# Block one's local attention takes q and k from the tiles that the pooled branch has already loaded

## The chip, the cores and the metric

The kernel runs on one core of a Trainium2 chip. The metric is the device time of one execution in microseconds (us), taken as the median of several runs; lower is better.

## The reference

The input is q, k and v of shape (4, 8, 576, 64): batch, heads, tokens, head size. Two attentions are added, and the sum goes through two feed-forward layers.

```
q_d, k_d, v_d = mean of q, k, v over groups of 4 tokens          # 144 pooled tokens
out_up    = repeat(softmax(q_d k_d^T / 8) v_d, 4 times)          # pooled branch
mask      = |i - j| < 4
out_local = softmax(where(mask, q k^T / 8, -1e9)) v              # local branch, a band of 7
x = (out_up + out_local) as (2304 tokens, 512)
h = x @ w_in1 (512 x 2048);  x = relu(h)^2 @ w_out1              # first layer
h = x @ w_in2;               out = (h * cos(h)) @ w_out2         # second layer
```

The two weight pairs come as 64-bit floats.

## The kernel before

Tokens are worked on in five blocks per layer; block one of the first layer has 512 tokens. For the first layer a slot is one of the 16 chunks of 128 hidden columns for one block: `stage_a` multiplies x by the chunk (L568), the activation follows, and `stage_b1` multiplies back into four accumulators (L620). Each operand is kept as a high part and a rest (`xh` and `xl`, `w1hi` and `loa`/`lob`, `gh` and `gl`), so a product is three matmuls.

**Attention.** Heads go in four pairs: heads 2p and 2p+1 lie on partitions 0-63 and 64-127. The pooled branch of a batch (`pool`) loads eight pieces of q and k (one per pair and tensor, 128 x 576) and four of v, and VectorE sums groups of four tokens (L260, L265, L267). `down` then makes pooled scores (L303), the exponentials on ScalarE (L277), transposes (L324, copies L331) and the product with v (L336, copies L345). The local branch goes by windows of 64 queries with up to 70 keys; block one has windows 0 to 7. `window` loads its own q and k (`qkw`, L367) and v (`vw`, L372). In `qkw` the two heads' queries stand side by side padded with zeros, so that one 128x128 weight tile gives the scores of both heads in one matmul per pair (L383), four per window, behind one matmul that writes the mask (L379). Then come the row maximum (L273), exponentials (L277), the scaling on GpSimd (L393), transposes (L403, copy L406), the product with v (L420), the sum with the pooled branch (L436), and its split in `xh` (L448) and `xl` (L449).

**Weights.** `conv1(f)` turns chunk f of the 64-bit weights into two 32-bit parts: the load `raw` (L461, two buffers), one pass on ScalarE (L475), four on VectorE (L477, L478, L482, L485), one on ScalarE that writes `w1hi` (L489), two on GpSimd (L496) and two stores (L521).

**Order.** Before the first slot all tasks of block one run in turn until they end (`early[0]` is true): `pool(0)`, its four `down`, windows 0 to 7, and the conversion of chunks 0 to 2; the warm-up matmuls (L697) stand between the turns. In that stretch the weight tiles `hi3` to `hi15` are still empty, and the buffers named in `SPREAD` use them: `need` takes an own buffer where there is one, or else one of the 13 empty tiles. A scheduler then sets the order on each engine, and each engine works its list strictly from front to back. SP issues all loads; all DMAs share the same 16 DMA engines.

Of the kernel before, what the change touches and what calls it, by code (L numbers as in the profile page):

```python
# [8 lines left out]
F32 = mybir.dt.float32  # L9
# [9 lines left out]
P = 128  # L19
B, H, S, D = 4, 8, 576, 64  # L20
# [3 lines left out]
HPAIR = H // 2  # L24
WQ = 64
WK = WQ + 2 * HALO
# [13 lines left out]
W0 = [sum(WINS1[:j]) for j in range(NB + 1)]  # L40
# [13 lines left out]
TOP_MIN = 2.0 ** -15  # L54
TOP_MAX = (2.0 - 2.0 ** -3 - 2.0 ** -23) * 2.0 ** 16
LO_RING = (("loa", AHEAD), ("lob", AHEAD + LAG))
SPREAD = ("pl", "qkw", "vw", "dpr", "dpt")
RANK = {"down": 0, "window": 1, "pool": 2, "conv1": 3, "conv2": 3}


# [8 lines left out]
def kernel(  # L69
# [43 lines left out]

    caps = {
        "a": 3, "h": 1, "acc": 4, "qkw": 3, "vw": 3, "pr": 3, "pt": 2, "xt": 1, "qp": 1, "xd": 2, "vp": 1, "av": 3, "pl": 2, "raw": 2,
        "dpr": 2, "dpt": 1,
    }
    used = dict.fromkeys(caps, 0)
    now = [-1]
# [3 lines left out]

    def need(name, n=1):
        while early[0] and name in SPREAD:
            if name != "pl" and used[name] < caps[name]:
                used[name] += 1
                held.setdefault(name, []).append(None)
                return
            if spare:  # L130
                held.setdefault(name, []).append(spare.pop(0))
                return
            yield
        while used[name] + n > caps[name]:
            yield
        used[name] += n

    def done(name, n=1):
        f = taken[name].pop(0) if early[0] and name in SPREAD else None
        if f is None:  # L140
            used[name] -= n
        else:
            spare.append(f)
# [4 lines left out]
    def task_tile(name, rows, cols):  # L148
        f = None
        if early[0]:  # L150
            f = held[name].pop(0)
            taken.setdefault(name, []).append(f)
        if f is None:
            return cm.tile([rows, cols], F32, tag=name, name=name, bufs=caps[name])
        return wp.tile([P, 2 * DM], F32R, tag=f"hi{f}", name=name).bitcast(F32)[:rows, :cols]
# [21 lines left out]


    pooled = {}
    xds = {}  # L180
    qk_used = {}
    vp_used = {}
# [5 lines left out]
    def pool(b):  # L188
        yield from need("qp")
        yield from need("vp")  # L190
        kp = cm.tile([P, HPAIR, SD], F32, tag="kp", name="kp", bufs=caps["qp"])
        vp = cm.tile([KTOK, 2, DM], F32, tag="vp", name="vp", bufs=caps["vp"])
        parts = [(i, hp) for hp in range(HPAIR) for i in range(2)]
        parts += [((0, 1), hp) for hp in range(HPAIR)] if early[0] else [((kt,), hp) for hp in range(HPAIR) for kt in range(2)]
        loaded = []
        for i, hp in parts:
            yield from need("pl")
            if isinstance(i, int):
                t = task_tile("pl", P, S)
                nc.sync.dma_start(out=t, in_=pool_qk[b, i, hp])  # L200
            else:
                t = task_tile("pl", KTOK, len(i) * FACTOR * P)
                nc.sync.dma_start(
                    out=t.rearrange("p (k c) -> p k c", k=len(i)),
                    in_=pool_v[b, hp, :, i[0]:i[-1] + 1],
                )
            loaded.append((i, hp, t))
            if len(loaded) < 2:
                continue
            if not early[0]:  # L210
                yield
            if b < PE_POOLED:
                if not early[0]:
                    yield
                bank, = yield from need_a()
                pe_pool(bank, loaded, kp, vp)
                done_a(bank)
                done("pl")
                done("pl")
                loaded = []  # L220
            while loaded:
                pool_sum(*loaded.pop(0), kp, vp)
                done("pl")
        pooled[b] = (qp, kp, vp)

    def pe_pool(bank, pieces, kp, vp):
# [25 lines left out]
    def pool_sum(*piece):  # L252
        with behind("gl", "xl"):
            pool_piece(*piece)
# [107 lines left out]
    def window(w):  # L362
        b, i, t0, k0, k1 = window_of(w)
        n, off = k1 - k0, HALO - (t0 - k0)
        yield from need("qkw")
        qk = task_tile("qkw", P, HPAIR * (2 * WQ + WK))
        nc.sync.dma_start(out=qk, in_=win_qk[w])  # L367
        qw = qk[:, :HPAIR * 2 * WQ].rearrange("p (h m) -> p h m", h=HPAIR)
        kw = qk[:, HPAIR * 2 * WQ:].rearrange("p (h s) -> p h s", h=HPAIR)
        yield from need("vw")  # L370
        vw = task_tile("vw", WK, DM)
        nc.sync.dma_start(out=vw, in_=win_v[w])  # L372
        yield
        if not early[0]:
            yield
        yield from need("pr")
        s, = yield from need_a()
        sv = s[:, :HPAIR * n].rearrange("p (h s) -> p h s", h=HPAIR)
        nc.tensor.matmul(  # L379
            sv, ident_b, band[:, off:off + n].unsqueeze(1).broadcast_to([P, HPAIR, n]), start=True, stop=False  # L380
        )
        for hp in range(HPAIR):
            last["pe"] = nc.tensor.matmul(  # L383
                sv[:, hp], qw[:, hp], kw[:, hp, :n], start=False, stop=hp == HPAIR - 1
            ).ins
        done("qkw")
        mx = cm.tile([P, 2, HPAIR], F32, tag="mx", name="mx", bufs=4)
        pr = cm.tile([P, HPAIR, WK], F32, tag="pr", name="pr", bufs=caps["pr"])
        prv = pr[:, :, :n]
        yield from exps(s, sv, mx, prv, SCALE)  # L390
        nc.vector.tensor_scalar_add(out=mx[:, 1], in0=mx[:, 1], scalar1=1e-9)
        nc.vector.reciprocal(out=mx[:, 1], in_=mx[:, 1])
        nc.gpsimd.tensor_tensor(  # L393
            out=prv, in0=prv, in1=mx[:, 1].unsqueeze(2).broadcast_to([P, HPAIR, n]), op=ALU.mult
        )
        yield
        if not early[0]:
            yield
        yield from need("pt")
        tp, = yield from need_a()  # L400
        tpv = tp.rearrange("p (h m) -> p h m", h=HPAIR)
        for hp in range(HPAIR):
            last["pe"] = nc.tensor.transpose(tpv[:n, hp], pr[:, hp, :n], ident).ins  # L403
        done("pr")
        pt = cm.tile([WK, HPAIR, P], F32, tag="pt", name="pt", bufs=caps["pt"])
        nc.scalar.copy(out=pt[:n], in_=tpv[:n])  # L406
        done_a(tp)
        yield
        while placed[0] < w:
            yield  # L410
        yield from need("av")
        j = max(n for n in range(NB) if W0[n] <= w)
        m = w - W0[j]
        while any((b, hp) not in downs for hp in range(HPAIR)):
            yield
        xh, xl = yield from x_tiles(j)
        av, = yield from need_a()
        avv = av.rearrange("p (h m) -> p h m", h=HPAIR)
        for hp in range(HPAIR):
            last["pe"] = nc.tensor.matmul(  # L420
                avv[:, hp], vw[:n, hp * P:(hp + 1) * P], pt[:n, hp], start=True, stop=True
            ).ins
        done("pt")
        done("vw")
        placed[0] += 1
        while any((b, hp) not in downs for hp in range(HPAIR)) or added[0] < w:
            yield
        if (j, m // 2) not in xts:
            yield from need("xt")
            xts[j, m // 2] = cm.tile([P, HPAIR, 2 * WQ], F32, tag="xt", name="xt", bufs=caps["xt"])  # L430
        xt = xts[j, m // 2]
        jd = WQ // FACTOR
        for a in range(2):
            rows = slice(a * D, (a + 1) * D)
            xa = xds[b][rows, :, i * jd:(i + 1) * jd].unsqueeze(3).broadcast_to([D, HPAIR, jd, FACTOR])
            nc.vector.tensor_tensor(  # L436
                out=xt[rows, :, (m % 2) * WQ:(m % 2 + 1) * WQ].rearrange("p h (j r) -> p h j r", r=FACTOR),
                in0=avv[rows, :, a * WQ:(a + 1) * WQ].rearrange("p h (j r) -> p h j r", r=FACTOR),
                in1=xa, op=ALU.add,
            )  # L440
        done_a(av)
        done("av")
        added[0] += 1
        if m % 2 or m == WINS1[j] - 1:
            m0 = m - m % 2
            cs = slice(m0 * WQ, (m + 1) * WQ)
            xv = xt[:, :, :(m % 2 + 1) * WQ]
            nc.scalar.activation(out=xh[:, :, cs], in_=xv, func=AF.Copy)  # L448
            last["xl"] = nc.vector.tensor_tensor(  # L449
                out=xl[:, :, cs], in0=xv, in1=xh[:, :, cs].bitcast(F32), op=ALU.subtract  # L450
            ).ins
            done("xt")
        ready.add(w)
# [453 lines left out]
```

## Time and profile before

| what | value |
|---|---|
| median of 3 runs | 1001.09 us (1000.05 to 1003.14) |
| the profiled execution | 1008.34 us, of which 1006.2 us is the span |
| TensorE (PE) matmuls busy | 966.9 us, 96% of the span |
| VectorE (DVE) / ScalarE (ACT) / GpSimd (POOL) busy | 613.0 / 462.7 / 146.0 us |
| moved by DMA | 145.50 MB, 145 GB/s over the span |
| granted TensorE clock, mean | 0.973 |
| first matmul of the first slot (L568) starts | 81.52 us after the span's start |

The busy share of an engine is a mean over stages that have different limits. A matmul in fp32 with weights is recorded as two matmul records. The clock of TensorE stands in the profile as the granted share: 1.00 is 2.4 GHz, 0.50 is 1.2 GHz.

### The profile page before, as it was taken

How to read it: one execution, taken by the hardware profiler on the slowest of the kernel's cores; microseconds unless marked ns; L12 is line 12 of the kernel's file. 1: busy time of each engine (PE TensorE's matmuls, PEld its weight loads, DVE VectorE, ACT ScalarE, POOL GpSimd, SP SyncE). 2: the span in 40 equal slices, each digit the busy share in tenths (PEclk: the TensorE clock that was granted, in tenths of full speed). 3: DMA queues.
4: the chain of work that ended last, by engine and by line, in shares of the span. 5: the costliest groups of instructions: out<-in, count | busy, mean ns of one | idle time of the engine just before them, and what ended most of it. 6: DMA issues, size and time to landing. Idle time of an engine off the chain costs nothing.

```text
span 1006.2 us, 13030 instructions
## 1 busy us (share of the span) xinstructions
PE 966.9 (96%) x4820; PEld 825.4 (82%) x4820; DVE 613.0 (61%) x1050; ACT 462.7 (46%) x865; POOL 146.0 (15%) x112
## 2 busy tenths in 40 slices
PE   6797998989999999999999999999999999999998
PEld 4586776869999999999999898888888888888887
DVE  5358999966456854345237836556556655655565
ACT  3544565535544644454345644344334433433343
POOL 1312654502110311211002600000000000000000
PEclk8679998999999999999999999999999999999999
DMA  9834676677568956586356756002000100100010
GB/s 253 285 113 148 228 251 240 222 226 270 169 209 266 315 179 208 173 303 239 106 187 247 273 167 246 1 0 84 1 1 21 43 1 0 43 1 1 1 43 22
DMA packets 55936, 145.50 MB, mean 145 GB/s; under 512 B 6664, under 2 KB 9864, under 8 KB 51520
## 3 DMA queue, kind: packets, MB, share of 16 engines
q1 hardware_dynamic: 55872, 144.67, 42.5%
q8 instruction: 38, 0.62, 0.3%
q14 instruction: 26, 0.21, 0.1%
HBM read 116.33 MB, written 28.31 MB: 144 GB/s over the span
## 4 chain that ended last, share of the span: by engine, by line
PE 74%; DVE 7%; issue 2%; DMA 2%; ACT 0%; SPq 0%; DVEq 0%
PE ps_h L568 35%; PE acc L626 20%; PE acc L620 14%; DVE bits L482 2%; PE ps_a L420 2%; PE ps_a L383 2%; DVE bits L478 1%; DVE gl L586 1%; PE ps_a L403 1%; DMA pl<-in_pool_qk_dram 1%; DMA pl<-in_pool_v_dram 1%; PE ps_a L336 1%; DVE bits L477 1%; PE ps_a L303 1%; DVE bits L485 1%
## 5 line engine op out<-in xcount | busy, mean ns | idle before, releaser
L586 DVE TENSOR_TENSOR gl<-gt,gh 128x448 fp32r<-128x448 f32 (+1 forms) x80 | 59.9, 749 | 116.1 <-ACT gh L580 96.3
L568 PE MATMUL ps_h<-xh,w1hi 128*128 128x448 f32 (+1 forms) x320 | 122.7, 384 | 6.1 <-ACT gt L591 5.4
L620 PE MATMUL acc<-gl,w1hi 128*128 128x448 f32 (+1 forms) x320 | 121.4, 379 | 2.4 <-DVE gl L586 2.2
L568 PE MATMUL ps_h<-xl,w1hi 128*128 128x448 f32 (+1 forms) x320 | 120.9, 378 | 0.8 <-DVE xl L449 0.8
L568 PE MATMUL ps_h<-xl,w2hi 128*128 128x512 f32 (+1 forms) x320 | 117.3, 373 | 0.0
L568 PE MATMUL ps_h<-xh,w2hi 128*128 128x512 f32 (+1 forms) x320 | 117.2, 373 | 0.0
L608 ACT ACTIVATE r<-r,half_pi 128x512 f32<-128x512 f32 (+1 forms) x80 | 54.6, 683 | 135.6 <-DVE r L604 135.6
L626 PE MATMUL acc<-w2hi,gh 128*128 128x512 f32 x288 | 113.7, 395 | 0.0
L626 PE MATMUL acc<-w2lo,gh 128*128 128x512 f32 x288 | 113.4, 394 | 0.0
L626 PE MATMUL acc<-w2hi,gl 128*128 128x512 f32 x288 | 113.4, 395 | 0.0
L620 PE MATMUL acc<-gh,w1hi 128*128 128x448 f32 (+1 forms) x320 | 104.2, 381 | 3.7 <-ACT gh L580 3.7
L602 DVE TENSOR_SCALAR u<-u 128x512 f32<-128x512 f32 (+1 forms) x80 | 32.0, 400 | 118.5 <-ACT u L597 118.1
L620 PE MATMUL acc<-gh,lo 128*128 128x448 f32 x256 | 93.7, 366 | 0.0
L591 ACT ACTIVATE gt<-ps_h 128x448 f32<-128x448 f32 (+1 forms) x80 | 44.1, 552 | 85.0 <-PE ps_h L568 84.0
L568 PE MATMUL ps_h<-xh,w2lo 128*128 128x512 f32 (+1 forms) x320 | 80.4, 371 | 0.0
L597 ACT ACTIVATE u<-ps_h,quarter 128x512 f32<-128x512 f32 (+1 forms) x80 | 51.6, 645 | 47.8 <-PE ps_h L568 47.6
L568 PEld LDWEIGHTS ps_h<-xh,w1hi 128*128 128x128 f32 x320 | 61.0, 191 | 13.8 <-ACT gt L591 6.5
L580 ACT ACTIVATE gh<-r 128x512 fp32r<-128x512 f32 (+1 forms) x80 | 47.1, 589 | 51.7 <-DVE r L612 46.8
L568 PEld LDWEIGHTS ps_h<-xh,w2hi 128*128 128x128 f32 x320 | 60.1, 188 | 12.2
L568 PEld LDWEIGHTS ps_h<-xl,w2hi 128*128 128x128 f32 x320 | 60.1, 188 | 12.2
L620 PEld LDWEIGHTS acc<-gl,w1hi 128*128 128x128 f32 x320 | 60.9, 190 | 10.8 <-DVE gl L586 4.3
L620 PEld LDWEIGHTS acc<-gh,w1hi 128*128 128x128 f32 x320 | 60.2, 190 | 11.0 <-ACT gh L580 4.8
(111 smaller groups left out, 1831.5 us busy)
## 6 DMA issues: line engine op xcount, KB each, us to landing
raw<-in_w_dram SPq DMA_DIRECT2D x32, 1024.0 KB
lo<-lo_d SPq DMA_DIRECT2D x128, 256.0 KB
qkw<-in_win_qk_dram SPq DMA_DIRECT2D x36, 396.0 KB
pl<-in_pool_qk_dram SPq DMA_DIRECT2D x32, 288.0 KB
w_d<-shi SPq DMA_DIRECT2D x10, 512.0 KB
w_d<-bits SPq DMA_DIRECT2D x10, 512.0 KB
w2lo<-w_d SPq DMA_DIRECT2D x10, 512.0 KB
w2hi<-w_d SPq DMA_DIRECT2D x10, 512.0 KB
```

The costliest lines, as they stand in the source:

```text
L383: last["pe"] = nc.tensor.matmul(sv[:, hp], qw[:, hp], kw[:, hp, :n], start=False, stop=hp == HPAIR - 1).ins
L420: last["pe"] = nc.tensor.matmul(avv[:, hp], vw[:n, hp * P:(hp + 1) * P], pt[:n, hp], start=True, stop=True).ins
L482: nc.vector.scalar_tensor_tensor(out=x, in0=low, scalar=29, in1=x, op0=ALU.logical_shift_right, op1=ALU.bitwise_or)
L568: nc.tensor.matmul(h[:, :n], a[:, c * P:(c + 1) * P], x[:, c, :n], start=i == 0, stop=i == len(order) - 1)
L580: nc.scalar.activation(out=gh, in_=gt, func=AF.Copy)
L586: last["gl"] = nc.vector.tensor_tensor(out=gl, in0=gt, in1=gh.bitcast(F32), op=ALU.subtract).ins
L591: last["relu"] = nc.scalar.activation(out=gt, in_=h, func=AF.Relu).ins
L597: nc.scalar.activation(out=u, in_=h, func=AF.Identity, bias=quarter, scale=float(1.0 / (2 * math.pi)))
L602: nc.vector.tensor_scalar(out=u, in0=u, scalar1=MAGIC, scalar2=MAGIC, op0=ALU.add, op1=ALU.subtract)
L608: nc.scalar.activation(out=r, in_=r, func=AF.Sin, bias=half_pi, scale=1.0)
L620: nc.tensor.matmul(acc[d][:, :n], a, x, start=f == 0 and i == 0, stop=f == NF - 1 and i == 2)
L626: nc.tensor.matmul(acc[t], x[:, ts], a[:, DM:2 * DM], start=f == 0 and i == 0, stop=f == NF - 1 and i == 2)
```

## The change

While `early[0]` holds, the eight q and k pieces of batch 0 are loaded in tiles named `qk0`, which have no buffers of their own and take eight of the 13 empty weight tiles. They are not given back after pooling but kept until all eight windows of block one have their scores. These windows load no `qkw` any more; each waits (in the program's order) until all eight pieces are requested, and slices its queries and keys out of them. As these queries are not padded, a pair's scores are made by two matmuls, one per head: 64 partitions, 64 weight columns, and the output on the head's own 64 partitions. Windows 8 and later are as before, and so are all later batches. All line numbers behind the edit grow, by 8 to 25 (L303 is L311, L331 is L339, L345 is L353, L461 is L486, L475 is L500, L489 is L514).

```
-SPREAD = ("pl", "qkw", "vw", "dpr", "dpt")
+SPREAD = ("qk0", "pl", "vw", "dpr", "dpt")
...
-        "dpr": 2, "dpt": 1,
+        "dpr": 2, "dpt": 1, "qk0": 0,
...
-            yield from need("pl")
-            if isinstance(i, int):
+            keep = early[0] and isinstance(i, int)
+            yield from need("qk0" if keep else "pl")
+            if keep:
+                t = whole[i, hp] = task_tile("qk0", P, S)
+                nc.sync.dma_start(out=t, in_=pool_qk[b, i, hp])
+            elif isinstance(i, int):
...
-                pool_sum(*loaded.pop(0), kp, vp)
-                done("pl")
+                piece = loaded.pop(0)
+                pool_sum(*piece, kp, vp)
+                if not early[0] or piece[:2] not in whole:
+                    done("pl")
...
+        apart = early[0]
+        if not apart:
...
...
+        while apart and len(whole) < 2 * HPAIR:
+            yield
         s, = yield from need_a()
...
+        if apart:
+            for hp in range(HPAIR):
+                for a in range(2):
+                    rows = slice(a * D, (a + 1) * D)
+                    last["pe"] = nc.tensor.matmul(
+                        sv[rows, hp], whole[0, hp][rows, t0:t0 + WQ], whole[1, hp][rows, k0:k1],
+                        start=False, stop=hp == HPAIR - 1,
+                    ).ins
+            scored.add(w)
+            if len(scored) == W0[1]:
+                for _ in range(2 * HPAIR):
+                    done("qk0")
+        else:
...
```

The scheduler's lists change in the first slots. On SP, the loads before, from the last window of block one on (`raw` is a 64-bit weight chunk, `pl` here the pooled branch of batch 1, `qkw` of windows 8 and later):

```order
L367 DMA qkw<-in_win_qk_dram 128x792
L372 DMA vw<-in_win_v_dram 70x512
L461 DMA raw<-in_w_dram 128x2048 x2
L200 DMA pl<-in_pool_qk_dram 128x576 x2
L367 DMA qkw<-in_win_qk_dram 128x792 x3
L461 DMA raw<-in_w_dram 128x2048
```

And SP after the change, from the pooled branch's v on:

```order
L209 DMA pl<-in_pool_v_dram 72x1024 x4
L382 DMA vw<-in_win_v_dram 70x512 x3
L486 DMA raw<-in_w_dram 128x2048 x2
L377 DMA qkw<-in_win_qk_dram 128x792
L206 DMA pl<-in_pool_qk_dram 128x576 x2
L377 DMA qkw<-in_win_qk_dram 128x792 x2
L382 DMA vw<-in_win_v_dram 70x512 x3
L486 DMA raw<-in_w_dram 128x2048
L377 DMA qkw<-in_win_qk_dram 128x792 x2
```

The first two weight chunks stood behind the q, k and v of all eight windows; now they stand behind the v of three.

ScalarE before, from the pooled queries' copies on (`dpr` and `pr` are the exponentials of the pooled and the local branch, `dpt` the transposed `dpr`, `xd` the pooled branch's output):

```order
L263 COPY qp<-qc 64x144 x8
L277 ACTIVATE dpr,dmx<-ps_acc,dmx 96x144 x12
L277 ACTIVATE pr,mx<-ps_acc,mx 128x67 x4
L277 ACTIVATE pr,mx<-ps_acc,mx 128x70 x8
L331 COPY dpt<-ps_acc 72x288 x4
L475 ACTIVATE bits<-raw 128x1024
L345 COPY xd<-ps_acc 64x144 x2
```

And ScalarE after:

```order
L271 COPY qp<-qc 64x144 x8
L285 ACTIVATE dpr,dmx<-ps_acc,dmx 96x144 x3
L500 ACTIVATE bits<-raw 128x1024
L285 ACTIVATE dpr,dmx<-ps_acc,dmx 96x144 x9
L500 ACTIVATE bits<-raw 128x1024
L285 ACTIVATE pr,mx<-ps_acc,mx 128x67 x4
L514 ACTIVATE w1hi_367<-bits 128x1024
L285 ACTIVATE pr,mx<-ps_acc,mx 128x70 x8
L339 COPY dpt<-ps_acc 72x288 x2
L500 ACTIVATE bits<-raw 128x1024
L353 COPY xd<-ps_acc 64x144 x2
```

The passes on chunks 0 and 1 have moved between the exponentials, and it is the pass on the third chunk that now stands ahead of the first copies of `xd`.

TensorE before, from the pooled branch's first products with v on (the weights of L403 are the exponentials of windows 0 and 1, L379 and L383 the mask and the scores of windows 3 and 4):

```order
L336 MATMUL ps_acc<-dpt,vp 128x288 x3
L324 MATMUL ps_acc<-const_sb,dpr 72x96 x3
L336 MATMUL ps_acc<-dpt,vp 128x288
L324 MATMUL ps_acc<-const_sb,dpr 72x96 x9
L403 MATMUL ps_acc<-const_sb,pr 67x128 x4
L403 MATMUL ps_acc<-const_sb,pr 70x128 x4
```

And TensorE after, from the same place on (`qk_164`, `qk_166` and so on are the eight kept pieces, q and k of each pair):

```order
L344 MATMUL ps_acc<-dpt,vp 128x288
L332 MATMUL ps_acc<-const_sb,dpr 72x96 x6
L344 MATMUL ps_acc<-dpt,vp 128x288
L428 MATMUL ps_acc<-const_sb,pr 67x128 x4
L428 MATMUL ps_acc<-const_sb,pr 70x128 x4
L391 LDWEIGHTS const_b
L391 MATMUL ps_acc<-const_b 128x280
L398 MATMUL ps_acc<-qk_166,qk_164 64x70 x2
L398 MATMUL ps_acc<-qk_175,qk_173 64x70 x2
L398 MATMUL ps_acc<-qk_184,qk_182 64x70 x2
L398 MATMUL ps_acc<-qk_193,qk_191 64x70 x2
```

Before, the transposes of all four pooled pairs stood ahead of windows 0 and 1; now only those of two pairs do, and windows 3 and 4 get their scores before the other two.

## Rows read from the trace of the kernel before

**Rows 1.** Stages: start:end, length, busy us per engine, granted clock, DMA share, GB/s

```profile
0.00:30.00 30.00, 20.67 (x100) 14.08 (x101) 17.91 (x42) 12.19 (x58) 5.57 (x11) 0.83 0.94 257
30.00:39.20 9.20, 3.98 (x26) 2.82 (x24) 0.66 (x3) 2.72 (x8) 1.26 (x2) 0.87 1.03 358
39.20:64.00 24.80, 24.11 (x97) 20.39 (x98) 10.43 (x21) 11.85 (x41) 3.80 (x4) 0.50 0.37 131
64.00:82.80 18.80, 15.42 (x118) 12.96 (x116) 16.92 (x41) 9.24 (x30) 6.25 (x7) 1.00 0.38 126
95.00:195.00 100.00, 93.53 (x436) 74.87 (x437) 97.03 (x125) 58.66 (x98) 54.07 (x31) 0.93 0.67 231
240.00:1006.20 766.20, 760.69 (x3788) 659.40 (x3786) 432.87 (x744) 342.66 (x587) 63.79 (x46) 1.00 0.35 120
```

The engines stand in the order PE, PE's weight loads, DVE, ACT, POOL.

**Rows 2.** Loads issued in the first 28 us: count, size of one

```profile
qkw<-in_win_qk_dram SPq DMA_DIRECT2D x8, 396.0 KB
pl<-in_pool_qk_dram SPq DMA_DIRECT2D x8, 288.0 KB
raw<-in_w_dram SPq DMA_DIRECT2D x2, 1024.0 KB
pl<-in_pool_v_dram SPq DMA_DIRECT2D x4, 288.0 KB
vw<-in_win_v_dram SPq DMA_DIRECT2D x8, 140.0 KB
```

**Rows 3.** Timeline: start, length, engine, line, tiles, count, [idle before <- releaser]

```profile
28.26 0.91 POOL L314 TENSOR_TENSOR dpr<-dpr,dmx 96x432 f32<-96x432 f32 x1 [0.93 <-ACT pr L277]
...
29.79 1.39 ACT L331 COPY dpt<-ps_acc 72x288 f32<-72x288 f32 x4
...
31.35 1.62 PE L336 MATMUL ps_acc<-dpt,vp 72*128 72x288 f32 x6
...
37.62 1.12 ACT L475 ACTIVATE bits<-raw 128x1024 f32<-128x1024 f32 x1 [6.44 <-DMA raw<-in_w_dram]
...
39.27 1.15 PE L324 MATMUL ps_acc<-const_sb,dpr 96*72 96x96 f32 x6 [5.29 <-issue]
...
46.42 1.91 PE L697 MATMUL ps_warm<-const_b 128*128 128x512 bf16 x4
```

**Rows 4.** Timeline from window 7's scores to the first slot's second product

```profile
66.47 1.01 PE L383 MATMUL ps_acc<-qkw 128*128 128x70 f32 x8
...
82.13 0.66 DVE L449 TENSOR_TENSOR xl<-xt,xh 128x512 fp32r<-128x512 f32 x1
...
85.82 0.33 SPq L461 DMA_DIRECT2D raw<-in_w_dram  x1
...
93.29 1.12 ACT L475 ACTIVATE bits<-raw 128x1024 f32<-128x1024 f32 x1 [3.00 <-DMA raw<-in_w_dram]
...
94.97 2.08 PE L620 MATMUL acc<-gh,w1hi 128*128 128x512 f32 x4 [3.29 <-ACT gh L580]
```

**Rows 5.** PE by line, 64 to 70 us (clock 1.00): busy us, mean ns of one

```profile
L420 PE MATMUL ps_acc<-pt,vw 70*128 70x128 f32 x22 | 3.0, 288 | 0.0
L383 PE MATMUL ps_acc<-qkw 128*128 128x70 f32 x16 | 2.0, 269 | 0.0
L697 PE MATMUL ps_warm<-const_b 128*128 128x512 bf16 x4 | 1.0, 379 | 0.0
L379 PE MATMUL ps_acc<-const_b 128*128 128x280 bf16 x2 | 0.6, 282 | 0.0
```

**Rows 6.** GpSimd, ScalarE and VectorE by line, first 95 us: busy us, mean ns of one

```profile
L496 POOL TENSOR_TENSOR loa<-bits,w1hi 128x512 fp32r<-128x512 f32 x3 | 3.8, 1267 | 16.3 <-ACT w1hi L489 16.3
L482 DVE SCALAR_TENSOR_TENSOR bits<-raw,bits 128x1024 uint32<-128x1024 uint32 x3 | 3.7, 1223 | 0.1
L489 ACT ACTIVATE w1hi<-bits 128x1024 fp32r<-128x1024 f32 x3 | 3.2, 1057 | 3.9 <-DVE bits L485 3.9
L478 DVE TENSOR_SCALAR bits<-bits 128x1024 uint32<-128x1024 uint32 x3 | 2.1, 694 | 0.1
```

More of the change, by code (lines that the diff above doesn't have):

```diff
@@ L125, in need @@
         while early[0] and name in SPREAD:
-            if name != "pl" and used[name] < caps[name]:
+            if name not in ("qk0", "pl") and used[name] < caps[name]:
                 used[name] += 1
@@ L179 @@
     pooled = {}
+    whole = {}
+    scored = set()
     xds = {}
@@ L364, in window @@
         n, off = k1 - k0, HALO - (t0 - k0)
[L365 to L369, printed above, removed]
+        apart = early[0]
+        if not apart:
+            yield from need("qkw")
+            qk = cm.tile([P, HPAIR * (2 * WQ + WK)], F32, tag="qkw", name="qkw", bufs=caps["qkw"])
+            nc.sync.dma_start(out=qk, in_=win_qk[w])
+            qw = qk[:, :HPAIR * 2 * WQ].rearrange("p (h m) -> p h m", h=HPAIR)
+            kw = qk[:, HPAIR * 2 * WQ:].rearrange("p (h s) -> p h s", h=HPAIR)
         yield from need("vw")
@@ L381, in window @@
         )
[L382 to L386, printed above, removed]
+        if apart:
[11 more added lines that the diff above has]
+        else:
+            for hp in range(HPAIR):
+                last["pe"] = nc.tensor.matmul(
+                    sv[:, hp], qw[:, hp], kw[:, hp, :n], start=False, stop=hp == HPAIR - 1
+                ).ins
+            done("qkw")
         mx = cm.tile([P, 2, HPAIR], F32, tag="mx", name="mx", bufs=4)
```

## The prediction, made before the changed kernel ran

> **What bounds the kernel now.** I read the table of stages first. From 240 us to the end TensorE's matmuls fill 760.7 of 766.2 us at the full clock [rows 1]: that part has nothing to give, and the change does not touch it. From 95 to 195 us VectorE is busy 97.0 of 100 us [rows 1] with the weight conversion; the change takes nothing from that list, but it can let it start sooner. What the change edits lies in the first 95 us, and there the limits differ from stage to stage. Until 39 us it is the loads: the DMA share is 0.94 up to 30 us and 1.03 up to 39.2 us [rows 1]. The timeline shows what waits for them: ScalarE stands idle 6.44 us for the first 64-bit weight chunk, which lands at 37.62, and TensorE stands idle 5.29 us behind ScalarE until 39.27 [rows 3]. From 39.2 to 64 us it is TensorE: busy 24.1 of 24.8 us, at clock 0.50 (1.2 GHz), while VectorE has 10.4 and ScalarE 11.9 us of work [rows 1]. From 64 us on the clock is 1.00 and VectorE leads, 16.9 of 18.8 us [rows 1]. Then a weight chunk is late once more: it is issued at 85.82, lands at 93.29 and keeps TensorE waiting 3.29 us [rows 4].
>
> So what counts is how far the second product of the first slot (94.97 us [rows 4]) moves. On VectorE, the lists of before and after hold the same conversions, pooling sums and window steps up to the first slot's `gl`, and agree row for row from about the 22nd slot on; I take it that a gain made by 95 us lasts to the end.
>
> **The loads.** Removed: eight `qkw` of 396 KB, 3.24 MB [rows 2]. Nothing is loaded instead, but five later `qkw`, two pieces of batch 1 and three `vw` now follow the first two weight chunks at once. Ahead of and with the first chunk, before: 0.10 MB constants, 3.54 MB pieces, 3.24 MB `qkw`, 1.15 MB `vw`, 1.05 MB chunk [rows 2] = 9.08 MB. By 37.6 us 257 GB/s x 30 + 358 GB/s x 7.6 = 10.4 MB had moved [rows 1], so its landing lags by the worth of 1.35 MB, since later loads move beside it. After: 0.10 + 3.54 + 0.43 (three `vw`) + 1.05 = 5.12 MB, at 257 GB/s 19.9 us without that lag and 25.2 with it; I take 22.5. The second chunk: 24 to 29 us. The third waits for a buffer that chunk 0 has been read out of (about 31 us), with 8.41 MB ahead of it: 9.46 to 10.8 MB, 34.9 to 38.7 us; I take 38, nearer to the lagging case that the trace shows.
>
> **ScalarE up to 39 us.** It gets the passes on chunks 0 and 1 between the exponentials, 2 x 1.12 [rows 3] + 1.06 for `w1hi` [rows 6] = 3.3 us, and some 0.7 us of waiting for chunk 0. Before, it was through with the exponentials at about 29.7 and with the four copies of L331 at 31.2 [rows 3]; after, with the exponentials and two copies at 34.4. Then it meets the third chunk, 38 + 1.1 = 39.1 us, against 37.62 + 1.12 = 38.7 before. ScalarE itself gains nothing here: the old wait has a successor about as late. The gain is in what was finished ahead of it: chunk 0 is converted, and windows 3 and 4 get scores on TensorE before it needs ScalarE again.
>
> **TensorE, windows 3 and 4.** They come behind window 1's transposes, which need GpSimd. VectorE now has chunk 0's four passes, 2 x 0.69 + 2 x 1.22 = 3.8 us [rows 6], between the small steps that GpSimd waits for; its fourth pooled scaling moves from 28.26 [rows 3] to 28.26 + 3.8 + 0.7 = 32.8, plus 0.9; then two window scalings (at most 0.9 each) and the two halves of chunk 0's rest (1.27 each [rows 6]): 38.0 us. Transposes of window 1: 0.5, so 38.5.
>
> The price of a window's scores is not in the trace: sixteen records of 64 x 64 weights for eight of 128 x 128. Eight of the old kind take 1.0 us at the full clock (16 in 2.0), 0.125 each, 0.27 from start to end [rows 5]. Below: half the columns and pairs side by side, 0.5 us. Above: no overlap at all, 16 x 0.27 = 4.3 us. The nearest row is the old one at its pace, so 1.0 (the two heads side by side) to 2.0 (one behind the other); I take 1.5, and 1.8 with the mask (0.3 [rows 5]). For windows 3 and 4: 3.6, and the warm-up 1.0 [rows 5]: 38.5 + 4.6 = 43.1, against 46.42 + 1.91 = 48.33 before [rows 3]: 5.2 us ahead.
>
> In the Trainium skill, "TensorEngine Tiling (Array Packing)", section Restrictions and Gotchas, different row tiles cannot access one PSUM bank at the same time, and both heads of a pair write the same bank here; no run shown has such a pair. By that rule the pair would be serial, 2.0 us for a window and some 2.5 us more over the five windows from 3 on than in my sum; if pairs overlapped, 2.5 us less.
>
> **TensorE, on to window 7's scores.** After that point its list holds 6 products with v of the pooled branch, two records each at 0.27 (six in 1.62 [rows 3]): 3.2; 12 transposes at 0.1 (0.19 at half clock [rows 3]): 1.2; windows 0 to 3 times v, 32 records at 0.136 (22 in 3.0 [rows 5]): 4.4; 12 transposes at the same price: 1.6; two warm-ups: 2.0; three windows' scores: 5.4. Together 17.8 us at the full clock: window 7 has its scores at 60.9 us, against 66.47 + 1.01 = 67.48 before [rows 4]: 6.6 us ahead. Before, most of the like list ran at 0.50, which it fell to in the idle stretch ahead of 39.27 and kept until 64 us [rows 1, 3]. Here TensorE has no gap like that by the reckoning above, so I take 1.00 from window 1's transposes on; that is the assumption on which most of the gain rests.
>
> **VectorE's tail.** From window 7's scores to the last `xl` of block one took 82.79 - 67.48 = 15.3 us [rows 4]. In the new list all passes on chunks 1 and 2 stand in that stretch, five more than before: 2 x 0.69 + 3 x 1.22 = 5.0 us [rows 6]. 1.9 us of idle in that stage (16.92 of 18.80 [rows 1]) can take a part, so 3.1 to 5.0; I take 3.1, as one window's sums also leave the stretch. `xl` is there at 60.9 + 18.4 = 79.3, 3.5 us ahead.
>
> **The late chunk.** Its buffer comes free at the last pass on chunk 2, which now stands three short steps ahead of that `xl`: issue at 77.8 instead of 85.82, landing 7.5 later (93.29 - 85.82 [rows 4]) at 85.3. From the pass on it to the second product took 94.97 - 93.29 = 1.7 us [rows 4]; the new list has three more passes between, each about half of 1.12 [rows 3], 1.7 together: 88.7. From `xl` alone it would be 79.3 + (94.97 - 82.79 - 3.29) = 88.2. The later holds: 88.7, 6.3 us ahead of 94.97.
>
> **The sum.** 1008.34 - 6.3 = 1002 us for the profiled execution. That one is 7.25 us above the median of the runs, 1001.09; I carry the difference over: 994.8 us, rounded 995. With 1.0 or 2.0 us for a window's scores, chunk 0 at 19.9 or 25.2 us, and 3.1 or 5.0 in the tail, each some 2 us, its own range is 990 to 998.
>
> **Rivals.** (1) Narrow scores at a low clock, slower. TensorE reaches window 1's transposes at 0.50 and does not come up to 1.00 before 64 us, as it did before. Then the 22.9 us of work from there costs 1.9 times as much (warm-ups 1.91 [rows 3] to 1.0 [rows 5]): by 64 us 25.5 us have done 13.4 of them, the other 9.5 follow at 1.00, window 7 is scored at 73.5, `xl` stands at 91.9 instead of 82.79, and 3.3 us of the late chunk's wait fall away: +5.8, 1007 us. It decides once more than half of that work runs at 0.50. For it: TensorE is idle before 22 us in both lists, and its clock was 0.50 from 39 to 64 although it was busy 24.1 of 24.8 us [rows 1]. Against it: a warm-up now stands ahead of the transposes too.
> (2) The loads stay the bound, no change. The third chunk lands at 41 or later because the loads of later windows fill the queue at once, and ScalarE and TensorE idle 4 to 5 us as before; the clock falls, and what the earlier chunk 0 gave is taken back: 998 to 1004, about 1001. For it: five `qkw` of later windows are issued in front of the third chunk. Against it: TensorE has two windows' scores to do in that time.
> (3) A larger gain: pairs side by side, chunk 0 at 20 us, full clock from 31 us on. Window 7 is scored 4 us sooner than in my sum, the late chunk with it: 988 to 990.
> That the change does not remove the loads is excluded by SP's list.
>
> **Chances.** Forecast 0.50, (1) 0.17, (2) 0.20, (3) 0.13. What can be told from no change is 0.3%, 3 us: below 998.1 lie nearly all of the forecast and all of (3), 0.61; within 3 us most of (2) and a rest of the forecast, 0.21; above 1004.1 all of (1) and a rest of (2), 0.18. The range reaches from 986, a little below (3), to 1004, the upper end of (2); outside it lie most of (1) and a little of (3).
>
> **What would show it.** The first pass on a weight chunk at 22 to 25 us instead of 37.6; ScalarE's longest wait for a chunk near 38 us and under 5 us; the clock at 1.00 between 39 and 64 us; eight narrow matmuls (16 records) in 1.0 to 2.0 us; window 7's scores at 58 to 63 us; the second product near 88.7; the stage from 95 us on of unchanged length. The forecast is wrong if the clock is 0.50 for most of 39 to 64 us, or if narrow matmuls cost over 3 us a window.

## The result, and the profile after

| | before | after |
|---|---|---|
| median of 11 runs each | 1001.09 us | 992.05 us |
| ratio of the runs | | 0.9901 [0.9877, 0.9925] |
| the profiled execution | 1008.34 us | 992.13 us |
| moved by DMA | 145.50 MB | 142.25 MB |
| the first slot's second product starts | 94.97 us | 84.43 us |

The changed kernel is 9.0 us faster by the medians and 16.2 us by the two profiled executions. Of 35 runs of the kernel before beside the first experiments, ten had a mean granted clock of 0.978 or less and took 1005.3 to 1013.1 us, the other 25 had 0.981 or more and took 997.8 to 1004.2, and the profiled execution (0.973, 1008.34 us) is of the first kind, so the difference of the two traces is larger than that of the medians.

The table of stages of the kernel after, in the columns of [rows 1]:

```profile
0.00:30.00 30.00, 20.05 (x124) 12.36 (x125) 19.83 (x43) 12.83 (x47) 5.05 (x10) 0.83 0.91 281
30.00:39.20 9.20, 6.87 (x56) 5.12 (x55) 3.03 (x4) 5.96 (x24) 5.04 (x6) 0.87 0.72 261
39.20:64.00 24.80, 21.25 (x192) 16.78 (x188) 16.25 (x46) 14.53 (x61) 2.61 (x4) 0.98 0.09 25
64.00:82.80 18.80, 16.87 (x75) 14.15 (x76) 15.42 (x27) 8.34 (x14) 10.10 (x8) 0.64 0.75 256
95.00:195.00 100.00, 91.17 (x446) 73.67 (x444) 94.11 (x130) 60.68 (x102) 49.97 (x34) 0.97 0.74 254
240.00:990.10 750.10, 744.58 (x3708) 647.28 (x3707) 425.53 (x728) 334.19 (x569) 59.98 (x43) 1.00 0.34 118
```

Against [rows 1]: up to 39 us the DMA share falls from 0.94 and 1.03 to 0.91 and 0.72. From 39.2 to 64 us the loads are all but over (0.09) and the clock is 0.98 where it was 0.50. From 64 to 82.8 us it is the other way round, 0.64 against 1.00. The last row spans 750.1 us where it was 766.2, but it also holds less (3708 records of TensorE for 3788), as the changed kernel is further on at 240 us; where the 16 us come from is read from the `gl` below.

The timeline of the kernel after, rows that answer to [rows 3, 4]; L500 is the first pass on a weight chunk, L398 a window's scores, L722 a warm-up, L474 the last `xl` of block one, L611 `gl`, L645 the second product:

```profile
21.77 1.13 ACT L500 ACTIVATE bits<-raw 128x1024 f32<-128x1024 f32 x1
...
35.32 1.12 ACT L500 ACTIVATE bits<-raw 128x1024 f32<-128x1024 f32 x1 [2.64 <-DMA raw<-in_w_dram]
36.98 1.04 PE L428 MATMUL ps_acc<-const_sb,pr 128*70 128x128 f32 x4 [2.33 <-issue]
...
40.56 1.04 PE L722 MATMUL ps_warm<-const_b 128*128 128x512 bf16 x4
...
54.09 0.70 PE L398 MATMUL ps_acc<-qk,qk 64*64 64x70 f32 x16
...
65.21 1.07 PE L428 MATMUL ps_acc<-const_sb,pr 128*70 128x128 f32 x4 [4.43 <-POOL pr L418]
...
71.80 0.33 SPq L486 DMA_DIRECT2D raw<-in_w_dram  x1
73.38 1.34 DVE L474 TENSOR_TENSOR xl<-xt,xh 128x512 fp32r<-128x512 f32 x1 [0.76 <-ACT xh L473]
80.23 2.14 ACT L500 ACTIVATE bits<-raw 128x1024 f32<-128x1024 f32 x2
84.29 0.68 DVE L611 TENSOR_TENSOR gl<-gt,gh 128x512 fp32r<-128x512 f32 x1
84.43 1.18 PE L645 MATMUL acc<-gh,w1hi 128*128 128x512 f32 x4
...
93.37 0.68 DVE L611 TENSOR_TENSOR gl<-gt,gh 128x512 fp32r<-128x512 f32 x1
...
550.49 0.61 DVE L611 TENSOR_TENSOR gl<-gt,gh 128x448 fp32r<-128x448 f32 x1
```

For the last rows, the same two `gl` in the kernel before, the first and the 73rd of 160 (`gl` is made once per slot, so it serves as a clock of progress):

```profile
94.95 0.69 DVE L586 TENSOR_TENSOR gl<-gt,gh 128x512 fp32r<-128x512 f32 x1 [3.39 <-ACT gh L580]
...
566.55 0.61 DVE L586 TENSOR_TENSOR gl<-gt,gh 128x448 fp32r<-128x448 f32 x1
```

The lead of the changed kernel is 10.7 us at the first `gl` (84.29), 14.3 at the 25th and 16.1 at the 73rd (550.49), and it stays there to the end of the span.

The first chunk is taken up at 21.77 with no wait (37.62 in [rows 3]), the idle of 6.44 us is 2.64, window 7 has its scores at 54.79 instead of 67.48 [rows 4], and the late chunk of [rows 4] is gone: both passes at 80.23 start without a wait. What is new is the idle of 4.43 us ahead of 65.21: TensorE is through with the scores so early that it waits for VectorE and GpSimd, and during that wait, at 64.1, the clock falls to 0.50.

The price of the narrow scores, in the PE groups by line from 48 to 56 us (clock 1.00; columns as in [rows 5]):

```profile
L445 PE MATMUL ps_acc<-pt,vw 70*128 70x128 f32 x24 | 3.2, 275 | 0.0
L398 PE MATMUL ps_acc<-qk,qk 64*64 64x70 f32 x48 | 2.1, 227 | 0.0
```

48 records in 2.1 us are 0.70 for a window; the eight wide ones took 1.0 [rows 5]. In the Trainium skill, "TensorEngine Tiling (Array Packing)", Restrictions and Gotchas would make the two heads of a pair serial, as they write one PSUM bank, and 2.0 us a window; the measurement does not bear that out. In its trace the second head's records start 6 to 7 ns behind the first's, each some 221 ns long. This fits the Trainium skill, "TensorE: Matmul & The Clock Gate", Part 3, by which tiles on different rows of the array overlap.

### The profile page after: what moved, and what is told of

The parts are those of the page before. It is cut to its first block, busy times and chain, and to the rows that moved or that the text cites. A ratio compares the mean times of both kernels' runs of the same rounds, so it can differ in the third digit from the quotient of the medians.

```text
span 990.1 us, 13151 instructions
## 1 busy us (share of the span) xinstructions
PE 954.4 (96%) x4888; PEld 815.9 (82%) x4888; DVE 613.2 (62%) x1050; ACT 463.2 (47%) x865; POOL 142.5 (14%) x112
## 2 busy tenths in 40 slices
DMA packets 54783, 142.25 MB, mean 144 GB/s; under 512 B 6536, under 2 KB 9736, under 8 KB 50368
## 4 chain that ended last, share of the span: by engine, by line
PE 78%; DVE 11%; DMA 5%; issue 3%; POOL 1%; ACT 1%; SPq 1%; POOLq 0%; DVEq 0%; ACTq 0%
PE ps_h L593 35%; PE acc L651 20%; PE acc L645 14%; DMA pl<-in_pool_v_dram 3%; PE ps_a L445 2%; DVE bits L507 2%; PE ps_a L408 2%; DVE bits L510 1%; DVE bits L503 1%; DVE gl L611 1%; PE ps_a L344 1%; DVE bits L502 1%; PE ps_a L428 1%; DMA raw<-in_w_dram 1%; DMA qkw<-in_win_qk_dram 1%
## 5 line engine op out<-in xcount | busy, mean ns | idle before, releaser
L611 DVE TENSOR_TENSOR gl<-gt,gh 128x448 fp32r<-128x448 f32 (+1 forms) x80 | 61.6, 770 | 108.3 <-ACT gh L605 92.1
L645 PE MATMUL acc<-gl,w1hi 128*128 128x448 f32 (+1 forms) x320 | 121.1, 378 | 6.6 <-DVE gl L611 6.4
L645 PE MATMUL acc<-gh,w1hi 128*128 128x448 f32 (+1 forms) x320 | 105.3, 379 | 2.1 <-ACT gh L605 2.1
L645 PE MATMUL acc<-gh,lo 128*128 128x448 f32 x256 | 93.2, 364 | 0.0
L593 PE MATMUL ps_h<-xh,w2lo 128*128 128x512 f32 (+1 forms) x320 | 80.4, 371 | 0.0
L645 PEld LDWEIGHTS acc<-gl,w1hi 128*128 128x128 f32 x320 | 60.5, 189 | 14.5 <-DVE gl L611 8.7
L593 PEld LDWEIGHTS ps_h<-xh,w2hi 128*128 128x128 f32 x320 | 60.2, 188 | 12.2
L593 PEld LDWEIGHTS ps_h<-xl,w2hi 128*128 128x128 f32 x320 | 60.1, 188 | 12.2
L645 PEld LDWEIGHTS acc<-gh,w1hi 128*128 128x128 f32 x320 | 60.1, 189 | 8.3 <-ACT gh L605 2.6
```

Of the source, the lines that this page charges most:

```text
L593: nc.tensor.matmul(h[:, :n], a[:, c * P:(c + 1) * P], x[:, c, :n], start=i == 0, stop=i == len(order) - 1)
L611: last["gl"] = nc.vector.tensor_tensor(out=gl, in0=gt, in1=gh.bitcast(F32), op=ALU.subtract).ins
L645: nc.tensor.matmul(acc[d][:, :n], a, x, start=f == 0 and i == 0, stop=f == NF - 1 and i == 2)
```

## The experiments

Two questions were open: which part of the change makes the gain, and whether a gain at the first slot lasts. The first four kernels undid or isolated a part each.

**e1: all eight loads back, unread.** Changed kernel, with each window's `qkw` loaded again in front of its `vw`; nothing reads it. Windows 0 to 2 load into `qkw` buffers, the others into those of `xh`, `xl` and `shi`.

```
...
+        if apart and w < 8:
+            nc.sync.dma_start(out=unread(w), in_=win_qk[w])
```

> The changed kernel with the eight loads of the windows' own q and k issued again (3.24 MB, into buffers that nobody reads), so only their bytes and their place ahead of the weight chunks come back; kept pieces and narrow matmuls stay. Theory 'loads' (the gain comes from the first weight chunks landing earlier, so that TensorE does not idle ahead of 39 us and its clock stays up): the first pass on a chunk waits until about 36 to 38 us again, time near that of before, ratio 0.996 to 1.002. Rival 'narrow matmuls' (the gain comes from sixteen 64x64 records costing 0.7 us where eight of 128x128 cost 1.0, times eight windows and twice at the low clock): the gain stays, ratio 0.990 to 0.993.

Measured: 1002.32 us, ratio to before 0.9996 [0.9963, 1.0029]. The whole gain is gone, as the loads theory expected.

**e2: only the narrow matmuls.** Kernel before, all its loads, per-head scores out of `qkw`.

```
-            last["pe"] = nc.tensor.matmul(
-                sv[:, hp], qw[:, hp], kw[:, hp, :n], start=False, stop=hp == HPAIR - 1
-            ).ins
+            for r in ([slice(0, D), slice(D, P)] if early[0] else [slice(0, P)]):
+                last["pe"] = nc.tensor.matmul(
+                    sv[r, hp], qw[r, hp, r] if early[0] else qw[:, hp], kw[r, hp, :n],
+                    start=False, stop=hp == HPAIR - 1,
+                ).ins
```

> The kernel before with its own loads, but the scores of windows 0 to 7 by one narrow matmul per head (64 rows, 64 columns) out of the window's own tile. Theory 'loads': 8 windows x 0.3 us at the full clock or 0.6 at the low one come off TensorE's stage from 39 to 64 us, 2 to 3 us at most: ratio 0.996 to 1.000. Rival 'narrow matmuls': ratio 0.990 to 0.993.

Measured: 1002.70, 1.0011 [0.9986, 1.0035]. Nothing from the narrow matmuls alone, it seemed.

**e3: half of the loads back.** As e1 with `w < 4`.

> The changed kernel with the q and k loads of windows 0 to 3 issued again, unread (1.62 MB). Theory 'loads': half the bytes, the first chunk lands some 5 us later than without, part of the gain is left: ratio 0.992 to 0.998, between the changed kernel (0.990) and the one with all eight. Rival 'narrow matmuls': 0.990 to 0.993 as with none. Rival 'place in the list' (what counts is whether the chunk stands ahead of the windows' loads, not how many bytes move): about as with all eight.

Measured: 1001.80, 0.9999 [0.9976, 1.0021]. A miss for the loads theory: half of the bytes took back everything. The rival 'place in the list' forecast that.

**e4: chunks first.** Kernel before, with the conversion tasks ahead of the windows, so that the first two chunks are requested first.

```
+    tasks += [conv1(0), conv1(1, 3), conv1(2, 6)]
     tasks += [window(w) for w in range(W0[1])]
-    tasks += [conv1(0), conv1(1, 3), conv1(2, 6)]
```

> The kernel before with all its bytes and its wide matmuls, but the conversion tasks stand ahead of the windows, so the first two weight chunks are loaded right behind the pooled branch's pieces and the windows' q, k and v behind them. Theory 'loads' in its strict form (the bytes themselves must go): windows 0 to 2 get their scores later by 2.1 MB, about 8 us, the stall moves from ScalarE to TensorE, ratio 0.998 to 1.006. Rival 'place in the list' (an early chunk is all that counts): most of the gain, ratio 0.990 to 0.994.

Measured: 998.39, 0.9977 [0.9960, 0.9993], between what the theories expected.

The traces did not fit the loads theory. e2 and e4 had their first `gl` at 85.0 and 80.4 us, about as early as the changed kernel (84.29), and lost it far behind the edit. The table of stages from 300 us on, of e2:

```profile
300.00:315.00 15.00, 13.08 (x76) 11.55 (x75) 9.73 (x19) 6.78 (x14) 0.65 (x1) 1.00 0.69 217
315.00:330.00 15.00, 13.84 (x76) 12.53 (x75) 10.81 (x19) 5.90 (x11) 3.04 (x2) 1.00 0.87 281
```

and of the changed kernel:

```profile
300.00:315.00 15.00, 15.00 (x92) 14.18 (x91) 12.13 (x22) 7.12 (x13) 0.65 (x1) 1.00 0.70 225
315.00:330.00 15.00, 14.95 (x78) 13.33 (x77) 11.69 (x25) 8.47 (x16) 4.61 (x3) 1.00 0.92 318
```

TensorE idles 3.1 us there in e2, in slots that no edit touches. What differs there is the instruction lists: the scheduler had ordered the later slots of e1, e2 and e4 otherwise (of VectorE's 1050 recorded instructions only the last 474 agree with the changed kernel's). So each edit had been measured together with a change of list. More or fewer warm-ups at the start change the list too, and four take only 1.04 us at 40.56 above; but their number is set per turn, and over eight or nine turns it adds up. By that the edits could be repeated with the changed kernel's list: in f1 the last 1002 instructions on VectorE agree with it, in f2 to f4 the last 933 (on every engine from the first `gl` on).

**f1: e1 with 30 first warm-ups for 32.**

> The changed kernel with all eight loads of the windows' q and k issued again but unread (2 of the 32 first warm-ups are left out, so that from the first slots on every engine has the changed kernel's list: the first kernel with these loads had another list from about 306 us on, and lost some 6 us there by its trace). If the loads make the whole gain: 998 to 1003 us. If half of what the first such kernel lost was only its later list: 994 to 998. If the narrow scores or the kept pieces make the gain: 990 to 994.

Measured: 994.68, 0.9935 [0.9907, 0.9962], in the range of 'half by its list'. The same loads as e1, 7.6 us faster. One of its twelve runs took 3965.49 us; without it the median is 994.61. Its profiled execution took 1004.16 us: 3.6 us behind the changed kernel at the first `gl` and 12.2 at the end, with the same list between. So a list does not fix the time of an execution.

**f2: e2 with 2 warm-ups between the turns for 4.**

> The kernel before with the first eight windows' scores made by one narrow matmul per head out of the windows' own loads, and nothing else of the change (2 warm-ups instead of 4 between the turns, which gives the later slots the changed kernel's list). If the loads make the gain: 998 to 1003 us, as they all stand ahead of the weight chunks here. If the list of the later slots made a part of it: 994 to 998. If narrow matmuls make it: 990 to 994.

Measured: 992.93, 0.9898 [0.9871, 0.9925]; e2 had 1002.70. It has 48 warm-ups for e2's 64, and its first `gl` comes 4.7 us sooner in the two traces (80.34 for 85.04), so the nudge is a part of this difference.

**f3: e4 with 3 warm-ups between the turns for 4.**

> The kernel before, wide scores and all its loads, but with the first weight chunks requested ahead of the windows' loads (3 warm-ups instead of 4 between the turns, which gives the later slots the changed kernel's list). If the gain is that the first two chunks arrive early: 989 to 995 us. If it is the bytes that are no longer loaded: 997 to 1002. The first such kernel came to 998.4 with another list from 306 us on that lost some 7 us by its trace; by that sum this one comes to about 992.

Measured: 991.53, 0.9889 [0.9859, 0.9919]; e4 had 998.39. This is the cleanest pair, as e4 is not behind at the first slot. The first and the 73rd `gl` of e4 and then of f3:

```profile
80.41 0.66 DVE L586 TENSOR_TENSOR gl<-gt,gh 128x512 fp32r<-128x512 f32 x1
...
557.87 0.61 DVE L586 TENSOR_TENSOR gl<-gt,gh 128x448 fp32r<-128x448 f32 x1
```

```profile
81.12 0.68 DVE L586 TENSOR_TENSOR gl<-gt,gh 128x512 fp32r<-128x512 f32 x1
...
550.29 0.61 DVE L586 TENSOR_TENSOR gl<-gt,gh 128x448 fp32r<-128x448 f32 x1
```

e4 loses 8.3 us on f3 between them, where no edit reaches and the order differs up to about the 65th slot; 4.1 of that comes behind the 25th `gl`, where the clock is 1.00 in both.

**f4: the kernel before with 8 warm-ups between the turns** (`WARM = 8`), no other edit.

> The kernel before with 8 warm-ups between the turns instead of 4, and with that the later slots' list of the changed kernel. If the low clock from 39 to 64 us was what cost the time, and more warm-ups lift it: 992 to 997 us, and the trace shows 1.00 there. If the clock was only a consequence of the late chunk: 999 to 1004, at a clock still near 0.50. If the later list makes a part of the gain whatever the front: 994 to 998.

Measured: 994.45, 0.9915 [0.9889, 0.9941]. Its weight chunks come as late as before the change, in the timeline of f4:

```profile
35.68 1.12 ACT L475 ACTIVATE bits<-raw 128x1024 f32<-128x1024 f32 x1 [0.60 <-DMA raw<-in_w_dram]
...
77.06 2.15 ACT L475 ACTIVATE bits<-raw 128x1024 f32<-128x1024 f32 x2
81.13 0.68 DVE L586 TENSOR_TENSOR gl<-gt,gh 128x512 fp32r<-128x512 f32 x1
...
551.03 0.61 DVE L586 TENSOR_TENSOR gl<-gt,gh 128x448 fp32r<-128x448 f32 x1
```

35.68 against 21.77 for the first chunk, and still the late pair of chunks finds no wait and the first `gl` comes 3.2 us ahead of the changed kernel's. f2 to f4 made nearly the whole gain with every load in place, so the loads theory fell as the main account. By their ranges f2 speaks for the narrow matmuls, f3 for the early chunks and f4 for the clock, but none of the three is in all of them; the list is. f4 alone mixes list and clock. h1 to h3 put one against the other.

**h1: the changed kernel with the list of before** (34 first warm-ups, 3 between, 61 in all for 68; VectorE's last 815 instructions agree with the kernel before, which is from the 13th slot on and not, as expected below, from the third or fourth).

> The changed kernel, with 34 first warm-ups for 32 and 3 between the turns for 4; by that alone the scheduler gives it the list of the kernel before from the third or fourth slot on, on every engine. If the gain is the list of the first 22 slots and not the front: 998 to 1003 us. If the front (fewer loads, early chunks) makes it: 990 to 994.

Measured: 998.66, 0.9956 [0.9931, 0.9981], 6.6 us slower than the changed kernel, whose interval lies wholly below: 0.9901 [0.9877, 0.9925]. The order of the instructions is the only thing that differs beside the seven warm-ups.

**h2: the changed kernel with e3's list** (30 first warm-ups; the last 1003 agree with e3). From the first `gl` on, this list is the changed kernel's own on every engine, in h2 and in e3; what they share apart from it stands ahead of that.

> The changed kernel with 30 first warm-ups for 32; by that alone it gets the list of the kernel with half of the loads back (1001.8 us) around the end of block one, where windows 8 and 9 are interleaved with the first slot otherwise than in the changed kernel. If that order made the half-loads kernel slow: 999 to 1003 us. If its loads did: 990 to 994.

Measured: 998.54, 0.9964 [0.9945, 0.9983]: just below the range of the list theory, far from the other. So most of what e3 lost is lost without its loads too, and goes with the order that it shares with h2 ahead of the first `gl`; the loads can account for the 3.3 us between the two, whose intervals overlap. The first and the 73rd `gl` of h2:

```profile
88.04 0.68 DVE L611 TENSOR_TENSOR gl<-gt,gh 128x512 fp32r<-128x512 f32 x1
...
556.86 0.61 DVE L611 TENSOR_TENSOR gl<-gt,gh 128x448 fp32r<-128x448 f32 x1
```

It is 3.8 us behind the changed kernel at the first and 6.4 at the 73rd, with one and the same list between: the later slots' list can't be what it lost by.

**h3: the kernel before with 6 warm-ups** (80 for 64 in all; the last 910 agree with the kernel before).

> The kernel before with 6 warm-ups between the turns for 4, which keeps its own list from the third or fourth slot on. Beside the kernel before with 8 warm-ups, which has the changed kernel's list and takes 994.5 us: if the list makes the difference, 998 to 1002 us here, without runs near 1008; if the clock in the front makes it, 993 to 997.

Measured: 998.29, 0.9953 [0.9928, 0.9978], no run above 999.7. The list theory's range; two more warm-ups in each turn are worth about 3 us. In the table of stages h3 has

```profile
39.20:64.00 24.80, 24.17 (x155) 19.84 (x153) 15.16 (x38) 15.49 (x57) 7.20 (x8) 0.85 0.55 183
```

and f4

```profile
39.20:64.00 24.80, 24.77 (x178) 19.72 (x178) 18.46 (x46) 16.52 (x58) 8.39 (x9) 1.00 0.60 211
```

so of the 3.8 us between h3 and f4 the clock can have a part, and by the single runs it can have all: three of h3's nine had a mean granted clock of 0.989 or 0.990 and took 993.8 to 995.1 us, the other six 0.981 to 0.984 and 997.7 to 999.7, while f4's six had 0.986 to 0.991 and took 992.5 to 996.6. h3 beside f4 does not tell list from clock. Between the changed kernel and h1 the clock has little (means 0.982 in both profiles).

**h4: both fronts.** Changed kernel with the chunks ahead of the windows too (24 first warm-ups; the last 1009 agree with the changed kernel), tried as a faster version.

> The changed kernel with the first weight chunks requested ahead of all windows' loads as well (24 first warm-ups for 32, which gives it the changed kernel's list to within a few rows). If the front carries through to the end: 986 to 989 us. If the later slots' list has given back by 550 us whatever the front is ahead, as with the kernels that reach the first slot 3 to 4 us sooner: 990 to 993.

Measured: 996.20, 0.9939 [0.9915, 0.9963]: slower than either range. Its lead at the first `gl` (83.1) is 1.2 us, and by the eighth slot it is 2.3 us behind. Why was not found out.

All kernels by the list of their later slots, as it stands in the traces:

| later slots' list | medians, us |
|---|---|
| the changed kernel's, from the first `gl` on | after 992.05; f1 994.68; f2 992.93; f3 991.53; f4 994.45; h4 996.20; h2 998.54; e3 1001.80 |
| that of before, up to about the 24th slot (h1 from the 13th on, h3 from the third or fourth); behind it the changed kernel's | before 1001.09; h1 998.66; h3 998.29 |
| a third, up to about the 65th slot | e1 1002.32; e2 1002.70; e4 998.39 |

The fastest six all have the changed kernel's list, and no kernel with another list is among them; but e3 and h2 have it too and are as slow as the others. So it goes with a short time and does not make one by itself: the order ahead of the first `gl` counts as well. The edits separate the kernels even less: all loads, half or none, early or late chunks, narrow or wide scores stand on both sides of 998 us.

## Why the prediction came out, and which step failed

The time and its direction came out (995.0 forecast, 992.05 measured), with a gain of 9.0 us for 6.3. The front went much as reckoned; the step behind it did not hold.

- **The loads.** The first chunk had landed by 21.77, at the early end of 19.9 to 25.2. The third chunk's pass ended at 36.44 instead of 39.1, behind a wait of 2.64 us: the successor to the wait that goes was named, 2.7 us too late. (Rival 2 counts five `qkw` in front of the third chunk; by SP's list there are three. And the row at 39.27 in [rows 3] names no engine that TensorE waited for: that it was ScalarE is inferred, from copies there that end at 39.17.)
- **Windows 3 and 4.** 41.60 (40.56 + 1.04) for 43.1.
- **Narrow scores**, the term that was mis-sized: 0.70 us a window for 1.5, half of it and below the whole range of 1.0 to 2.0. Over the five windows from 3 on that is some 4 us, and most of why window 7 was scored 6 us sooner than forecast (54.79 for 60.9). Rival 3, at 988 to 990, had that part.
- **The clock.** 0.98 from 39 to 64 us, as assumed; rival 1 is out. That a TensorE so far ahead would idle 4.43 us at 61, with the clock at 0.50 from 64.1 to 77.8, was not seen.
- **VectorE's tail** took 19.9 us (54.79 to 74.72) for 18.4; `xl` 74.7 for 79.3.
- **The late chunk.** Issued at 71.80 for 77.8; no wait. The second product at 84.43 for 88.7, 10.5 us ahead for 6.3.
- **"I take it that a gain made by 95 us lasts to the end"** is the step that failed. In the two traces that the sum is about, the gain at the first `gl` is 10.7 us and grows to 14.3 at the 25th and to 16.1 at the 73rd. (The clock can have a part in that: from 95 to 195 us it was 0.93 before and 0.97 after.) The lists of the two kernels differ up to about the 24th slot, and I took them as worth the same because they hold the same work. h1, the same edit in another order, loses 6.6 us by the medians. Its first, third and 73rd `gl`:

```profile
79.63 0.68 DVE L611 TENSOR_TENSOR gl<-gt,gh 128x512 fp32r<-128x512 f32 x1
...
90.63 0.68 DVE L611 TENSOR_TENSOR gl<-gt,gh 128x512 fp32r<-128x512 f32 x1
...
551.70 0.61 DVE L611 TENSOR_TENSOR gl<-gt,gh 128x448 fp32r<-128x448 f32 x1
```

  In its profiled execution, its fastest (993.12), it is 4.7 us ahead of the changed kernel at the first and 1.2 behind at the 73rd. h3, profiled at its median (998.29), has

```profile
82.71 0.66 DVE L586 TENSOR_TENSOR gl<-gt,gh 128x512 fp32r<-128x512 f32 x1
...
95.09 0.73 DVE L586 TENSOR_TENSOR gl<-gt,gh 128x512 fp32r<-128x512 f32 x1
...
556.65 0.61 DVE L586 TENSOR_TENSOR gl<-gt,gh 128x448 fp32r<-128x448 f32 x1
```

  against 84.29, 93.37 and 550.49: ahead by 1.6, then behind by 1.7 and by 6.2. With both executions at their kernels' medians, 4.4 of the 6.2 us come behind the third slot.

  Where the old order loses shows in part: from the tenth to the 25th `gl` the three traces with the list of before take 1.3 (h1), 3.7 and 3.8 us longer than the changed kernel, the seven others with the changed kernel's list between 1.5 less and 0.6 more. Behind the 25th, where these eleven kernels have one list, they still differ: 283.2 us to the 73rd in the changed kernel, 284.5 to 288.7 in the others. f4 shows the same with the changed kernel's list alone: 3.2 us ahead at the first `gl`, 0.5 behind at the 73rd.
- **Carrying 7.25 us over** was the second weak step. The clock of 0.50 in [rows 1], on which most of the forecast gain rested, may be missing in the median run: 24.8 us at 0.50 take 0.012 off the mean clock of 1006 us, and the profiled execution's mean of 0.973 is 0.010 below the 0.983 in the middle of the 35 runs. That is an estimate; no trace of a median run of before is there to show it. Where the stretch is missing, the change cannot win it back.

So that the forecast came near is in part luck: it set the front's gain at 6.3 us where the traces have 10.5, it left out what the order of the later slots adds, and it carried a gain read from one execution over to the median. By the medians 6.6 us of the 9.0 go with the order (h1 to after) and 2.4 with the rest of the change (before to h1; f4 to after is 2.4 too, and putting the loads back at one list costs 2.6 in f1 and 3.3 in e3 against h2; but f3, with every load in place and wide scores, is 0.5 us faster than the changed kernel). Each of these has an interval of some 2.5 us either way, and h3 has about as much from two warm-ups a turn, so that the front's part is not settled to better than a few microseconds. Nor is it settled how the 6.6 us divide between the order ahead of the first slot and the order behind it: h2, which differs from the changed kernel in two warm-ups and in the first of these alone, loses 6.5. TensorE's waits from 90 to 240 us sum to 13.4 us in h3 and 12.3 in the changed kernel, and no single one is the difference. The loss behind the first slot is plain for the third list alone, 8.3 us from e4 to f3; the idle time from 300 to 330 us in e2 is a part of that, though the trace of f1, with the changed kernel's list, has 2.8 us of it near there too.

A small part that goes with the edit itself does show. From the 36th to the 61st `gl` TensorE idles nowhere, and outside the third list all kernels have the same list there; the four that load no `qkw` for windows 0 to 7 (the changed kernel, h1, h2, h4) take 149.6 to 149.9 us, the seven that load any take 151.3. In some of these slots the same matmuls follow each other every 200 ns instead of 206. Why was not found out.

## What to carry to other kernels

Where a scheduler orders the whole program, an edit at the start also draws a new order, and that may be worth more than the edit (here 6.5 to 9.8 us between kernels that differ in 2 to 16 warm-ups alone). Compare the lists from the edit to the end before crediting it, and repeat an experiment with a small nudge that gives both kernels the same list; then look at a marker such as the first `gl`, to see what the nudge itself does. And see whether the profiled execution is of the kind that the median is: its mean clock beside that of the other runs tells.

## What the runs showed of the hardware

- Sixteen records of 64x64 weights, two heads on separate halves of the partitions and in one PSUM bank, take 0.70 us at clock 1.00, 1.20 at 0.50 (38.18 in the changed kernel); eight of 128x128 took 1.0 at 1.00.
- In the changed kernel the clock fell from 1.00 to 0.50 at 64.1 us, in an idle stretch of 4.43 us, and was back at 1.00 at 77.8; TensorE was busy 11.9 of the 13.7 us between.
